# One written order for the whole program of a fused attention and gated MLP kernel, with VectorE and GpSimd placed instruction by instruction and every tile at a written place

## The chip, the cores and the metric

One core of one Trainium2 chip runs the whole program. The metric is the device time of one execution in microseconds (us); the figures for a version are the median, lowest and highest of its runs. The core has five engines that matter here: PE (TensorE; "PEld" are its weight loads, which overlap its matmuls), DVE (VectorE), ACT (ScalarE), POOL (GpSimd), and SP, which issues nearly all transfers between DRAM and on-chip memory. Each engine works its own list of instructions strictly in order; an instruction waits until the data and the places it needs are free, and everything behind it on that engine waits too.

## What is computed

Eight batches with eight heads of dimension 64 hold 512 local and 32 global tokens each. A local token attends to the 32 global tokens and to its local neighbours within 32 positions; a global token attends to all 544. The 4608 results, 512 values each, go through an RMSNorm and a gated MLP with 1536 inner columns:

```python
s_g = scale * q_g @ k_all.T ; out_g = sm(s_g) @ v_all
s_l = concat([scale * q_l @ k_g.T, where(|i-j| <= 32, scale * q_l @ k_l.T, -1e9)])
out_l = sm(s_l) @ concat([v_g, v_l])
xn  = x / sqrt(mean(x * x) + 1e-6) * rms_g
g   = xn @ w_gate ; silu = g * (1 / (1 + exp(-g)))
out = (silu * (xn @ w_val)) @ w_out
```

Inputs and outputs are fp32.

## The kernel before

**Tiles.** The tokens are worked in nine chunks: chunks 0 to 7 are the 512 local tokens of one batch each, chunk 8 is the 256 global tokens. The sigmoid is formed by a tanh. Every large fp32 operand is split into two f16 parts, high and low, so that one product is three f16 matmuls (names `xh`, `xl` for the input, `wf`, `wo` for the weights). Chunks 0 and 1 multiply plainly (`first_chunk`, `moe_f`; matmuls of 128x512 into `p`). Chunks 2 to 7 use a form with seven products in place of eight on quarters of the matrices: `moe_pair` does seven products of 12 matmuls 128x256 for each of six pairs of gate and value columns (into `pq`), `moe_out` the like for the output weight (into `pr`). The combined weights for that are made once, by `fold` and `fold_out`, stored in DRAM (`wd`, `wa`, `wb`) and loaded again for every chunk in tiles `wt` (`fetch`) and `wu` (`fetch_out`).

**Stages.** A head of some 172 us loads and converts the weights, does the attention of chunks 0 and 1 and all of chunk 0's MLP. Then, chunk by chunk, the MLP of one chunk runs on PE, with the attention of a later chunk and the loads of weights between its products. In the head, step names are a letter and a number: L loads a unit (two heads) of q and k, V of v, S scores, M mask and row minimum (DVE), E exponentials (ACT), T transposes (PE), C copies, A values, X division, N and D norm factors, U, H and Y the transposed and split input, I a half product, O the output products. `E5.1` is the exponential of unit 5, half 1. In the chunks, `P24` is the product of work item 24, `R24` what follows it on the other engines, `t` its tail, `w` a load or store, `n` the norm, `O` an output product, and the steps of an attention unit are L, S, M, E, N, F, D, T, V, A, B, X, Y for local tokens (`local_halves`) and GL, GS, GM, GN, GT, GV, GA, GD, GX for global ones (`global_unit`: scores, mask, exponential, transposes, ...).

**Order.** The kernel runs under a manual schedule: what stands earlier in the program stands earlier on its engine. In the head the string `ORDER` lists whole jobs and each is called at once (L1904). For chunks 1 to 8 every step is first recorded (`write`, `doing`), and then replayed by a string for that chunk (`_ORDER_1` to `_ORDER_8`; all calls come from L1929, which is why most rows of the profile name that line). A step is cut into pieces `.0`, `.1` where the engine changes, or at every instruction for the steps R, t and n. So a chunk's steps cannot mix with another chunk's, nor the head's with chunk 1's, and a step of several DVE instructions (a mask, a norm) is one entry.

**Places.** Tiles come from rotating pools, one tag for each kind: `wf` 12 buffers of 128x1024 words, which also hold `wt`, `wu`, `vv` and more, `wo` 7, `h` 6, `st` 6, `v` 4 and so on. The eight PSUM banks are divided by tag too: `pa` 4, `po` 2, `pg` 1, `pv` 1 (`attn_bank` gives one of the four of attention). A new tile waits for the last reader of the one that had its buffer.

## Time and profile before

| | |
|---|---|
| time, median of 3 runs | 920.26 us (919.47 to 922.45) |
| span of the profiled execution | 922.7 us |
| PE busy | 878.8 us, 95% |
| DVE busy | 724.5 us, 79% |
| ACT busy | 556.3 us, 60% |
| POOL busy | 273.2 us, 30% |
| mean DMA rate | 230 GB/s |

The profile holds one execution; the span is its own time, from its first to its last instruction, and no other time of that execution was taken. It lies 2.4 us above the median of the runs. Times in the rows below count from the start of the span. An engine's idle time has a releaser, the instruction or transfer that ended it. PE's granted clock is given as a share of full speed: 1.00 is 2.4 GHz, 0.50 is 1.2 GHz. Where a row of the timeline ends in square brackets, the first number is how long the engine had stood idle before it, and the name behind the arrow is what released it.

### The profile page before, as it was taken

The numbers are of one execution on the slowest core, as the hardware profiler recorded it, in microseconds if no ns is written. First come the engines' busy times: TensorE is split into PE (matmuls) and PEld (weight loads), VectorE is DVE, ScalarE is ACT, GpSimd is POOL, SyncE is SP. The second block draws the span as 40 slices with busy tenths as digits, with TensorE's granted clock in tenths as the row PEclk, the third lists the DMA queues.
The fourth block names the chain that finished last, engine by engine and source line by source line (L and its number), as shares of the span: only waits on it lengthen the run. The fifth ranks groups of instructions, "written<-read, shape, count | busy, mean of one in ns | idle before, by whom it ended". The sixth has DMA issues, their size and how long they took to land.

```text
span 922.7 us, 27756 instructions
## 1 busy us (share of the span) xinstructions
PE 878.8 (95%) x11430; PEld 671.4 (73%) x11430; DVE 724.5 (79%) x1831; ACT 556.3 (60%) x1341; POOL 273.2 (30%) x244
## 2 busy tenths in 40 slices
PE   5699989999999999999999999898999999999998
PEld 4644445544547886588888888787888888888887
DVE  6899998868796887877987888587887897777554
ACT  6899995636452755457565767466575862456132
POOL 0000000032435776306440244122520454133311
PEclk9699989999999999999999999999999999999999
DMA  9983615495377869686677769667876666888665
GB/s 337 405 301 106 192 47 173 130 333 174 90 248 243 274 206 300 194 257 233 206 258 263 245 222 293 198 208 243 265 250 223 206 222 244 247 246 273 215 232 191
DMA packets 101006, 212.03 MB, mean 230 GB/s; under 512 B 8080, under 2 KB 34448, under 8 KB 100880
## 3 DMA queue, kind: packets, MB, share of 16 engines
q1 hardware_dynamic: 100448, 209.94, 69.5%
q8 instruction: 89, 1.46, 0.6%
q10 hardware_dynamic: 432, 0.33, 0.1%
q14 instruction: 37, 0.30, 0.1%
HBM read 183.24 MB, written 27.00 MB: 228 GB/s over the span
## 4 chain that ended last, share of the span: by engine, by line
PE 40%; DVE 5%; DMA 3%; ACT 3%; issue 2%; POOL 1%; DVEq 0%; ACTq 0%; POOLq 0%; SPq 0%
PE pq L1929 20%; PE pr L1929 14%; PE p L1929 3%; DMA wt<-wd 2%; ACT e L1929 1%; PE a L1929 1%; DVE v L1929 1%; DMA wu<-wb 1%; DVE s L1929 1%; DVE u L1929 1%; POOL hs L1929 1%; POOL hu L1929 1%; PE s L1929 1%; ACT s L1929 1%; DVE t L1929 1%
## 5 line engine op out<-in xcount | busy, mean ns | idle before, releaser
L1929 PEld LDWEIGHTS <-wt 128*128 128x128 f16 x3312 | 322.7, 98 | 56.9 <-issue 11.1
L1929 PE MATMUL pq<-xh,wt 128*128 128x256 f16 x1152 | 206.6, 274 | 6.8 <-DMA wt<-wd 2.5
L1929 PE MATMUL pq<-ht,wt 128*128 128x256 f16 x1296 | 158.0, 274 | 2.1 <-POOL ht L1929 1.2
L1929 PE MATMUL pq<-xl,wt 128*128 128x256 f16 x576 | 157.8, 274 | 0.1
L1929 ACT ACTIVATE e<-e,sm 128x128 f32<-128x128 f32 x288 | 104.2, 390 | 27.8 <-DVE sm L1929 27.8
L1929 POOL TENSOR_TENSOR hu<-v,hu 128x256 f16<-128x256 f32 (+1 forms) x60 | 56.5, 958 | 177.6 <-ACT hu L1929 155.1
L1929 PE MATMUL pr<-wu,hs 128*128 128x256 f16 x792 | 92.4, 273 | 0.3 <-DVE hs L1929 0.3
L1929 POOL TENSOR_TENSOR e<-e,sm 128x512 f32<-128x512 f32 x24 | 27.7, 1162 | 205.3 <-DVE sm L1929 205.3
L1929 PEld LDWEIGHTS <-hs 128*128 128x128 f16 x792 | 77.4, 98 | 9.7 <-DVE hs L1929 0.6
L1929 POOL TENSOR_TENSOR hs<-u,hs 128x512 f16<-128x512 f32 x50 | 60.5, 1228 | 65.6 <-ACT hs L1929 37.9
L1929 PE MATMUL pr<-wu,hu 128*128 128x256 f16 x594 | 70.8, 273 | 1.0 <-DMA wu<-wb 0.6
L1929 DVE TENSOR_TENSOR s<-pq,s 128x512 f32<-128x512 f32 x66 | 44.9, 685 | 29.9 <-PE pq L1929 14.1
L1929 ACT ACTIVATE t<-u,half_inv 128x512 f32<-128x512 f32 x72 | 49.6, 717 | 27.0 <-DVE u L1929 23.0
L1929 DVE SCALAR_TENSOR_TENSOR t<-t,u 128x512 f32<-128x512 f32 x72 | 54.0, 758 | 14.4 <-ACT t L1929 14.3
L1929 ACT COPY s<-pq 128x512 f32<-128x512 f32 x72 | 41.3, 580 | 38.3 <-DVE s L1929 18.2
L1929 PEld LDWEIGHTS <-hu 128*128 128x128 f16 x594 | 57.6, 98 | 8.6 <-DMA wu<-wb 0.9
L1929 DVE TENSOR_TENSOR v<-pq,s 128x512 f32<-128x512 f32 x72 | 49.0, 683 | 18.6 <-PE pq L1929 14.8
L1929 PE MATMUL po<-wo,h 128*128 128x512 f16 x288 | 63.4, 379 | 0.0
L1651 PE MATMUL p<-xh,wf 128*128 128x512 f16 x192 | 58.8, 379 | 3.1 <-DVE t L1763 1.2
L1929 PE MATMUL p<-xh,wf 128*128 128x512 f16 x192 | 59.8, 385 | 0.5 <-DVE t L1929 0.5
L1651 PEld LDWEIGHTS <-wf 128*128 128x128 f16 x288 | 27.7, 98 | 37.0 <-issue 3.1
L1929 PEld LDWEIGHTS <-wf 128*128 128x128 f16 x288 | 27.8, 99 | 34.6 <-issue 2.9
(380 smaller groups left out, 1704.7 us busy)
## 6 DMA issues: line engine op xcount, KB each, us to landing
wt<-wd SPq DMA_DIRECT2D x120, 512.0 KB, 5.3
wu<-wb SPq DMA_DIRECT2D x36, 512.0 KB, 5.3
wr<-in_w_in_dram SPq DMA_DIRECT2D x24, 512.0 KB, 8.7
wu<-wa SPq DMA_DIRECT2D x24, 512.0 KB, 4.7
k<-in_qkb_dram SPq DMA_DIRECT2D x24, 448.0 KB, 6.5
gkq<-in_gkq_dram SPq DMA_DIRECT2D x16, 576.0 KB, 7.1
wt<-wd SPq DMA_DIRECT2D x36, 256.0 KB, 4.2
v<-in_vb_dram SPq DMA_DIRECT2D x24, 352.0 KB, 5.6
```

The costliest lines, as they stand in the source:

```text
L1651: nc.tensor.matmul(ps[:, :n], rows[:, a, o : o + P], ch[z][k][:, :n], start=(k == 0 and i == 0), stop=(k == NK - 1 and i == 2),)
L1929: return lambda *a, **k: write(self.engine, lambda: call(*a, **k))
```

## The change

The number of instructions of each kind does not change: 8693 matmuls and transposes, 1543 DVE, 1049 ACT and 240 POOL instructions and 494 transfers from SP are called in both versions. What changes is their order and the places of their tiles.

- The nine tables become one, `ORDER`, over the whole program, with names `chunk:step.n`. The head's steps are recorded and replayed like those of the chunks (chunk number 0), so that any entry may stand anywhere: the head's last work between chunk 1's, a chunk's loads in the chunk before. The old head string stays as `JOBS` and only says in which order steps are recorded.
- Every DVE and every POOL instruction is an entry of its own.
- The pools go. 43 tiles `page` (128x1024 words), 8 tiles `wide` (128x1152) and 8 `banks` are made once, and `tile_of` and `bank_of` take the place of each tile from the written lists `PAGES` and `BANKS`. Any bank may serve any purpose.
- The transposed global weights of `global_unit` are held in two tiles, `pt` and `end`, since one of five parts is longer than a page.
- The scratch for DMA descriptors is set to 2048 bytes (`dynamic_dma_scratch_size`).

The core of the diff; of the tables it shows a piece each:

```diff
-ORDER = """
-z0 L0 S0 M0.0 M0.1 L1 S1 M1.0 E0.0 M1.1 E0.1 T0.1 T0.0 W0 m0 s0 E1.0 C0.0 z1 l0 g0 L2 S2 M2.1 T1.0
+ORDER = """
+0:L0.0 0:S0.0 0:M0.0.0 0:M0.0.1 0:M0.0.2 0:M0.0.3 0:E0.0.0 0:L2.0 0:L3.0 0:M0.1.1 0:M0.1.0 0:M0.1.3
...
-_ORDER_5 = """
-R16.0 N3/2+1.0 w10.0 P18.0 R18.0 t10.3 GV/1+1.0 w13.0 t12.0 t17.1 t18.0 R17.0 D1/2+1.0 V/2+1.0 P19.0
+4:w55.0 4:T1/0+2.0 4:O37.0 4:T3/0+2.0 4:O38.0 4:O39.0 4:n49.1 4:n50.0 4:O40.0 4:R59.0 5:w13.0
...
+PAGES = """
+0c 0a 1a 0a 1a 5a 6a 0a 6a 7a 8a 15a 5a 2a 3a 2a 11a 12a 6c 5a 2c 4a 19a 1c 2c 9a 10a 18a 13a 3a 4a
...
+BANKS = """
+0 1 3 5 0 4 3 2 3 5 3 0 4 1 0 6 2 1 3 4 5 2 1 0 4 4 0 1 5 4 1 5 5 4 2 3 1 0 5 7 2 1 0 5 5 7 6 3 1 7
...
-    pool = ctx.enter_context(tc.tile_pool(name="pool", bufs=2))
+    page = [con.tile([P, 1024], F32, tag=f"page{i}", name=f"page{i}") for i in range(NPAGE)]
+    wide = [con.tile([P, 1152], F32, tag=f"wide{i}", name=f"wide{i}") for i in range(NWIDE)]
+    banks = [psum.tile([P, 512], F32, tag=f"bank{i}", name=f"bank{i}") for i in range(8)]
+    page_at, bank_at, smalls = iter(PAGES.split()), iter(BANKS.split()), [0]
+    def tile_of(shape, dt, name):
...
+        at = next(page_at)
+        if n > 1024:
+            t = wide[int(at[1:])][:, :n]
+        else:
+            of, i = (wide, at[1:-1]) if at[0] == "W" else (page, at[:-1])
+            q = ord(at[-1]) - ord("a")
+            t = of[int(i)][:, q * 256 : q * 256 + n]
...
+    def bank_of(name):
+        return banks[int(next(bank_at))]
...
-            pt = pool.tile([P, 2, 5, P], F32, tag="gpt", bufs=1, name=f"gpt{b}")
+            pt = tile_of([P, 2, 4, P], F32, f"gpt{b}")
+            end = tile_of([P, 2, P], F32, f"gpe{b}")
...
-        t = pool.tile([P, 2, 2, 2, HT], F16, tag="wf", bufs=NF, name=f"wt{c}_{g}{i}")
+        t = tile_of([P, 2, 2, 2, HT], F16, f"wt{c}_{g}{i}")
...
-                st["ps", p] = psum.tile(
-                    [P, 512], F32, tag=bank[p], bufs=2 if bank[p] == "po" else 1, name=f"pq{p}_{g}"
-                )
+                st["ps", p] = bank_of(f"pq{p}_{g}")
...
-        if on and (on != engine or step[0] in "Rtn"):
+        if on and (on != engine or engine in ("vector", "gpsimd") or c and step[0] in "Rtn"):
...
-    for c, plan in plans.items():
-        for name in orders.get(c, plan):
-            for call in plan.pop(name) if c in orders else plan[name]:
-                call()
+    for name in ORDER.split() or list(plan):
+        for call in plan.pop(name):
+            call()
...
-    nc = bacc.Bacc("TRN2", target_bir_lowering=False, num_devices=1)
+    nc = bacc.Bacc("TRN2", target_bir_lowering=False, num_devices=1, dynamic_dma_scratch_size=2048)
```

Three places show how the order moves. The first is ACT in the head, around the exponentials of unit 5 (`E5.1` writes `e_1524`, `E5.0` writes `e_1539`), for which PE's transposes T5.1 and T5.0 wait. Before:

```order
L485 ACTIVATE wr_1475<-wr_1475 128x512
L485 ACTIVATE wr_1477<-wr_1477 128x512
L476 ACTIVATE w17t<-wr_1481 128x512
L476 ACTIVATE w17t<-wr_1483 128x512
L737 COPY pt_1544<-t_1514 128x512
L509 ACTIVATE wq_1555,rowsq<-w16t 128x1024
L509 ACTIVATE wq_1570,rowsq<-w14t 128x1024
L737 COPY pt_1544<-t_1574 128x512
L717 ACTIVATE e_1524,sm_1263<-e_1524,sm_1263 128x128 x4
```

After, `E5.1` is the row on `page_63` and `E5.0` the one on `page_81`; `rowsq` marks the squares of an output weight, 128x1024 each:

```order
L2088 ACTIVATE wide_108<-wide_106 128x512
L2088 ACTIVATE wide_108<-wide_107 128x512
L2088 ACTIVATE page_103<-bank_114,half_inv 128x512
L2088 ACTIVATE page_85<-page_67 128x512
L2088 ACTIVATE page_85<-page_87 128x512
L2088 ACTIVATE page_63,sm_20_181<-page_63,sm_20_181 128x128 x4
L2088 COPY page_72<-bank_116 128x512
...
L2088 ACTIVATE page_76,rowsq<-page_92 128x1024
L2088 ACTIVATE page_80,rowsq<-wide_108 128x1024
L2088 ACTIVATE page_80,rowsq<-page_85 128x1024
L2088 ACTIVATE page_81,sm_20_181<-page_81,sm_20_181 128x128 x4
```

The two squares that stood right ahead of `E5.1` now stand behind it, ahead of `E5.0`, whose own predecessors before were three squares behind `E5.1`.

The second is PE in chunk 1, from the global scores (GS, the rows of 32x272) to their transposes (GT, the rows with `ident`), which need the mask on DVE and the exponential on ACT in between. Before, with 12 matmuls of one gate column between the two:

```order
L1929 MATMUL gs_2275<-gkq_2260 32x272
L1929 MATMUL gs_2277<-gkq_2260 32x272
L1929 LDWEIGHTS wf_1133
L1929 MATMUL p_6_2288<-xh_2169,wf_1133 128x512
...
L1929 MATMUL p_6_2288<-xh_2193,wf_1133 128x512
L1929 MATMUL gt_2295<-ident,ge_2273 112x128 x4
```

After, with three times 12 matmuls, into three banks:

```order
L2088 MATMUL bank_120<-wide_108 32x272
L2088 MATMUL bank_115<-wide_108 32x272
...
L2088 MATMUL bank_114<-page_94,page_65 128x512
...
L2088 MATMUL bank_116<-page_94,page_65 128x512
...
L2088 MATMUL bank_121<-page_94,page_101 128x512
...
L2088 MATMUL bank_120<-ident,wide_108 112x128 x4
```

Two more columns' worth of products moved in between scores and transposes.

The third is SP around the transfer of the weight tile `wt_31` of chunk 5 (entry `w13` of that chunk), which its product P23 reads. Before, behind the global values `gv` of chunk 5's own unit:

```order
L1929 DMA wt_32_3022<-wd_100 128x2x1024
L1929 DMA wt_22_2996<-wd_99 128x2x1024
L1929 DMA wt_23_3006<-wd_99 128x1024
L1929 DMA gv_2987<-in_gv_dram 112x1024
L1929 DMA gv_2988<-in_gv_dram 112x512
L1929 DMA wt_31_3016<-wd_100 128x2x1024
```

After it is the row into `page_88`, ahead of the loads of the global keys and queries (`gkq`) for the unit that is worked in chunk 5:

```order
L2088 DMA page_70<-wd_152 128x2x1024
L2088 DMA page_88<-wd_155 128x2x1024
L2088 DMA wide_109<-in_gkq_dram 128x1152
L2088 DMA wide_110<-in_gkq_dram 128x1152
L2088 DMA page_89<-in_gv_dram 112x1024
```

The transfer moved from the middle of chunk 5 to the end of chunk 4.

## Rows read from the trace of the kernel before

**Rows 1.** The page: busy time of each engine over the span, with its share and its count of instructions, and the granted clock of PE in 40 equal slices, in tenths.

```profile
PE 878.8 (95%) x11430; PEld 671.4 (73%) x11430; DVE 724.5 (79%) x1831; ACT 556.3 (60%) x1341; POOL 273.2 (30%) x244
PEclk9699989999999999999999999999999999999999
```

**Rows 2.** Busy time by stretch: from and to in us, length, then busy us (and instructions begun) of PE, PE's weight loads, DVE, ACT and POOL, the granted clock, the DMA engines' busy share and GB/s. The first four stretches are the head, the next chunk 1, the last chunk 7.

```profile
0.00:44.00 44.00, 27.16 (x601) 23.44 (x602) 32.42 (x148) 33.90 (x100) 0.20 (x4) 0.77 0.98 370
44.00:112.00 68.00, 64.87 (x493) 31.48 (x493) 67.31 (x137) 65.70 (x104) 0.00 (x0) 1.00 0.61 205
112.00:132.00 20.00, 15.50 (x235) 9.16 (x234) 17.85 (x64) 18.29 (x43) 0.00 (x0) 0.83 0.25 90
132.00:172.00 40.00, 40.00 (x491) 22.95 (x492) 33.76 (x80) 24.29 (x63) 0.00 (x0) 1.00 0.34 113
172.00:286.00 114.00, 110.67 (x1184) 55.09 (x1165) 90.80 (x241) 56.59 (x168) 40.83 (x32) 0.99 0.68 210
783.00:874.00 91.00, 90.95 (x1012) 79.86 (x1010) 65.35 (x130) 41.39 (x72) 29.58 (x28) 1.00 0.77 243
```

**Rows 3.** PE's longest waits, summed by line and releaser: us in total, times, longest.

```profile
PE x00t L1110 <- DVE dg L1104: 6.3, 1, 6.3
PE s L688 <- DMA k<-in_qk_dram: 6.1, 1, 6.1
```

**Rows 4.** PE's timeline in the head, start and length in us: the transposes T5.1 and T5.0.

```profile
120.17 1.48 PE L732 MATMUL t<-ident,e 128*128 128x128 f32 x4 [3.05 <-ACT e L717]
128.38 0.92 PE L732 MATMUL t<-ident,e 128*128 128x128 f32 x4 [1.12 <-DVE sm L702]
```

**Rows 5.** PE's timeline in chunk 1: the transposes GT.

```profile
208.92 0.76 PE L1929 MATMUL gt<-ident,ge 128*112 128x128 f32 x5 [2.34 <-ACT ge L1929]
209.94 0.82 PE L1929 MATMUL gt<-ident,ge 128*112 128x128 f32 x5 [0.26 <-ACT ge L1929]
```

**Rows 6.** PE's timeline, the waits of over 0.3 us for a weight transfer in chunks 2 to 8: P41 of chunk 4, P23 and P33 of chunk 5, O18 of chunk 8.

```profile
550.88 1.49 PE L1929 MATMUL pq<-ht,wt 128*128 128x256 f16 x12 [0.65 <-DMA wt<-wd]
627.14 0.39 PE L1929 MATMUL pq<-xh,wt 128*128 128x256 f16 x1 [2.21 <-DMA wt<-wd]
643.75 0.28 PE L1929 MATMUL pq<-xh,wt 128*128 128x256 f16 x1 [0.31 <-DMA wt<-wd]
910.49 0.72 PE L1929 MATMUL pr<-wu,hu 128*128 128x256 f16 x5 [0.64 <-DMA wu<-wb]
```

**Rows 7.** PE's timeline, the waits of over 0.3 us for another engine's work in chunks 1 to 5 (GT's apart): in order, a product of chunk 1, P30 of chunk 2, P3 and P29 and O36 of chunk 3, P19 of chunk 4, P4 of chunk 5.

```profile
183.41 0.38 PE L1929 MATMUL p<-xh,wf 128*128 128x512 f16 x1 [0.47 <-DVE t L1929]
333.14 0.27 PE L1929 MATMUL pq<-xh,wt 128*128 128x256 f16 x1 [0.65 <-DVE u L1929]
391.45 0.81 PE L1929 MATMUL pq<-ht,wt 128*128 128x256 f16 x6 [1.24 <-POOL ht L1929]
434.31 0.27 PE L1929 MATMUL pq<-xh,wt 128*128 128x256 f16 x1 [1.45 <-ACT u L1929]
483.85 0.93 PE L1929 MATMUL pr<-wu,hu 128*128 128x256 f16 x7 [0.38 <-DVE oo L1929]
518.48 0.27 PE L1929 MATMUL pq<-xh,wt 128*128 128x256 f16 x1 [1.25 <-DVE s L1929]
595.39 0.27 PE L1929 MATMUL pq<-xh,wt 128*128 128x256 f16 x1 [0.32 <-DVE s L1929]
```

**Rows 8.** PE's timeline in chunk 5: the values of a local unit, behind a wait that the trace gives no releaser.

```profile
587.86 0.42 PE L1929 MATMUL a<-et,v 32*64 32x64 f32 x21 [2.18 <-issue]
```

**Rows 9.** The five stretches behind the head's first 44 us in which PE's granted clock was 0.50, columns as in rows 2.

```profile
121.80:125.20 3.40, 3.40 (x128) 2.89 (x112) 2.19 (x14) 3.40 (x11) 0.00 (x0) 0.50 0.03 5
128.60:132.00 3.40, 3.40 (x11) 1.50 (x10) 3.33 (x7) 2.80 (x6) 0.00 (x0) 0.50 0.18 71
210.50:213.90 3.40, 3.40 (x34) 1.43 (x39) 0.86 (x3) 1.54 (x4) 0.00 (x0) 0.50 0.57 160
589.40:592.80 3.40, 3.40 (x18) 2.36 (x17) 0.30 (x1) 1.32 (x4) 0.00 (x0) 0.50 0.99 266
626.90:630.30 3.40, 3.16 (x15) 2.24 (x16) 0.31 (x1) 3.35 (x14) 0.51 (x1) 0.50 0.99 295
```

**Rows 10.** ACT's timeline ahead of T5.1: the last square of an output weight, then the first exponential of E5.1.

```profile
118.10 1.06 ACT L509 ACTIVATE wq<-w14t 128x1024 bf16<-128x1024 f32 x1
119.61 0.42 ACT L717 ACTIVATE e<-e,sm 128x128 f32<-128x128 f32 x1
```

**Rows 11.** The chain of work that ended last, a piece of it: start, length, what; 13 products of 12 matmuls in a row on PE.

```profile
518.48 17.38 PE pq L1929 x156
```

**Rows 12.** The page's list of transfers (KB each, median us from issue to landing), for the weight tiles.

```profile
wt<-wd SPq DMA_DIRECT2D x120, 512.0 KB, 5.3
```

**Rows 13.** DVE's and POOL's timeline in chunk 2: a DVE instruction with two on-chip operands beside POOL, the two of POOL that it met, a DVE instruction that reads PSUM beside POOL, and the first form again where POOL did nothing.

```profile
336.96 1.27 POOL L1929 TENSOR_TENSOR s<-s,s 128x512 f32<-128x512 f32 x1
337.24 1.54 DVE L1929 SCALAR_TENSOR_TENSOR t<-t,u 128x512 f32<-128x512 f32 x1
338.19 2.58 POOL L1929 TENSOR_TENSOR od<-os,od 128x1024 f16<-128x1024 f32 x1
339.33 0.65 DVE L1929 TENSOR_TENSOR u<-pq,s 128x512 f32<-128x512 f32 x1
298.35 0.68 DVE L1929 SCALAR_TENSOR_TENSOR t<-t,u 128x512 f32<-128x512 f32 x1
```

More of the change, by code (lines that the diff above doesn't have):

```diff
@@ L794, in load @@
             if w == 0:
-                late["mask"] = con.tile([P, 6 * P], F32, tag="mask", name="maskb")
+                late["mask"] = tile_of([P, 6 * P], F32, "maskb")
                 nc.sync.dma_start(late["mask"], maskb)
@@ L885, in scores @@
             st["et"] = [
-                pool.tile([P, 1088], F32, tag="k", name=f"et{u}{x}") for x in range(2)
+                tile_of([P, 1088], F32, f"et{u}{x}") for x in range(2)
             ]
@@ L1374, in products @@
             hi, lo = ch["op"][p]
-            first = p in bank
+            first = p in own
             for j in range(2):
```

839 lines of the change are left out of this document (487 added, 352 removed), and 8 rows, old and new, of the table BANKS.

## Prediction

> **What bounds the kernel now.** I read the page first. PE is busy 95% of the span and no other engine over 80% [rows 1]; since the change keeps every matmul, the most that it can give back is what PE stands idle, 922.7 − 878.8 = 43.9 us, and what PE loses where its clock is low. Busy time by stretch then says where the idle time lies [rows 2]: 16.8 us in the first 44 us, 3.1 us to 112 (68 less 64.87), 4.5 us from 112 to 132, none from 132 to 172, 3.3 us in chunk 1, and at the end almost none: chunk 7 runs at 90.95 of 91 us. So chunks 6 and 7 have nothing to give, the head and chunks 1 to 5 something. [...]
>
> PE's waits and its timeline give the single stalls. Two large ones stand at the start: 6.1 us for the first keys and 6.3 us for a norm factor of chunk 0 [rows 3]. Then 3.05 us ahead of T5.1 and 1.12 us ahead of T5.0 [rows 4], 2.34 and 0.26 us ahead of the global transposes of chunk 1 [rows 5], four waits for weights [rows 6], seven for another engine [rows 7], and one of 2.18 us without a releaser [rows 8]. The granted clock is the third source: behind the start it fell to 1.2 GHz in five stretches [rows 9], each with PE busy for all or nearly all of its 3.4 us, so each did 1.7 us' worth of work at 2.4 GHz and cost about 1.7 us. Each follows one of the stalls above: in order T5.1, T5.0, GT, the wait of 2.18 us, and P23's 2.21 us. I count such a stretch as gone when its stall goes.
>
> **The change, part by part.** Only order and places change; I priced every instruction in both orders at the mean of its shape in this trace and compared what stands ahead of each waiting instruction on its engine. All terms are against the profiled execution's span, 922.7 us, which lies 2.4 us above the median of 920.26; I carry the sum to both.
>
> *A, unit 5 in the head.* Before T5.1, ACT ran two squares of 1.06 us each and only then E5.1 [rows 10]; they now stand behind it. All told ACT's work ahead of E5.1 falls from 105.8 to 95.9 us, but ahead of E5.0 only from 110.5 to 108.3. T5.0 comes behind T5.1 on PE with the same PE work ahead of it (97.9 us in both), so what T5.1 gains beyond E5.0's own 2.2 us is waited for again at T5.0. Late next is E5.0. Bounds: 0, since DVE is 90% and ACT 91% busy there [rows 2], and −7.6, both stalls and both clock stretches (4.17 + 3.4). I take −2.2, E5.0's own advance, and leave the stretches, since half of the idle time stays.
>
> *B, global transposes of chunk 1.* GT waited for ACT's exponential behind 12 matmuls of 128x512. Matmuls of 128x256 run at 17.38 / 156 = 0.111 us each where nothing waits [rows 11]; twice that for 512 columns makes 12 of them 2.7 us. The time from scores to transposes was then 2.7 + 2.6 = 5.3 us. Now 36 matmuls, 8.0 us, stand between. The stall should go with its clock stretch: −4.3 (2.6 + 1.7). Bounds 0 (the mask, now split into entries, falls behind other DVE work) and −4.3. The cover is those three products; without them the 2.6 us return.
>
> *C, weight transfers.* The four waits sum to 0.65 + 2.21 + 0.31 + 0.64 = 3.81 us [rows 6]. A tile of 512 KB lands 5.3 us after its issue [rows 12]. I counted PE's work between a transfer's entry and its first product: 63 of 222 transfers had under 5.3 us before, 2 of 221 have now, and the median went from 8.0 to 42.5 us. For the four that waited it went 0.1 to 13.1, 2.7 to 43.3, 0.1 to 37.7 and 6.0 to 74.7. A free place must exist that early, and SP's queue is in order, so a transfer that waits for its page holds those behind it; with 8 to 40 us in hand that is survivable. −5.5, the waits and P23's clock stretch; bounds 0 and −5.5.
>
> *D, engines that were late.* The seven waits sum to 0.47 + 0.65 + 1.24 + 1.45 + 0.38 + 1.25 + 0.32 = 5.76 us [rows 7]. The time table is meant for these: a DVE instruction with two on-chip operands took 1.54 us beside two of POOL and 0.68 us alone, while one that reads PSUM took 0.65 us beside POOL [rows 13]. Only the DVE and POOL waits can come from that; the 1.45 us stood behind ACT's own queue. I take half, −2.9; bounds 0 and −5.8.
>
> *E, the wait without releaser* (2.18 us and its clock stretch [rows 8, 9]): nothing in the order tells its cause, so 0; bounds 0 and −3.9.
>
> *F, the start:* the norm factor's chain (row sums, scale, spread) is the same length, and its DVE work ahead 0.7 us shorter (26.9 to 26.2): 0, bounds −2 and +1. Its loads end as before, so the 6.1 us for the keys stay.
>
> *G, banks.* With eight free banks in place of 4 + 2 + 1 + 1, a bank is not always given back earlier. I counted PE work between the last product into a bank and the first into the next tile there: of 525 such turns 44 left under 1.4 us before, 65 do now. Six of the waits above (all of [rows 7] but POOL's) were such turns: 4.52 us, so 0.103 us for each of the 44. 21 more cost +2.2; bounds 0 and the rival below.
>
> Sum: −2.2 − 4.3 − 5.5 − 2.9 + 2.2 = −12.7, that is 910.0 for an execution like the profiled one, **907.6 us** for the median.
>
> [...] By [rows 13] a DVE instruction beside POOL was longer by 0.86 us, less than POOL's 1.27. [...]
>
> **Rivals.**
> 1. *The table only moves the wait.* If DVE is held anyway for as long as POOL works, standing the two in turn frees no time on DVE: the products' results come out of the banks as late as before, and D is 0. For it: in [rows 13] POOL's 1.27 us had 0.99 left when DVE began, and DVE's 0.68 grew by 0.86, nearly a full wait. Against: an order can put PSUM readers, which lose nothing, beside POOL. 907.6 + 2.9 = **910.5**. [...]
> 2. *More goes.* The wait of 2.18 us (E, 3.9) and the rest of A's stalls with one clock stretch (4.17 − 2.2 + 1.7 = 3.7) go too, and the banks cost nothing (2.2): 907.6 − 9.8 = **897.8**. For it: nothing else bounds PE behind 172 us. Against: DVE's and ACT's load in the head.
> 3. *The idle time returns elsewhere, or the order on paper does not hold on the chip:* the head's middle is bound by DVE (17.85 of 20 us [rows 2]), transfers wait for pages rather than for their turn, and gaps as large as the old ones open at other products. **920 ± 2.**
> 4. *Slower: bank turns.* Place: the products of `moe_pair` and `moe_out`, one every 1.34 us (12 x 0.111), each of which needs a bank that DVE or ACT must have read out. The order was made from durations written in a table; where DVE runs an instruction late, the 65 tight turns all wait, and since DVE is now fixed instruction by instruction, nothing else of its own can fill in. Price: mean of the six, 4.52 / 6 = 0.75 us. It decides from 20 more waiting turns on (14.9 / 0.75, the gains of A to D); if half of the 65 wait, 24.4 us against 4.5 paid now, +19.9 − 14.9 = +5: **925**. For it: more tight turns than before, and a table rests on durations, where one form took 0.68 or 1.54 us [rows 13]. Against: 38 of 44 did not wait.
>
> **How the numbers follow.** A difference of 0.3% (2.8 us) is about what a measurement can tell. Forecast 0.39, rival 1 0.15, rival 2 0.10, rival 3 0.15, rival 4 0.21. The first three are faster by over 0.3%: 0.64; rival 3 is the same: 0.15; rival 4 slower: 0.21. The range goes from 897, just below rival 2 (the bounds of A to E together, 27.1, would give 893), to 926, just above rival 4 with half of the tight turns waiting; its worse outcomes and all bounds at once are left out, under 2 in 10. Faster cases alone span 897 to 917.
>
> **What would show it.** Right: PE busy about as before (879 us) and idle near 31 us; no wait of over 1 us at GT in chunk 1; no wait for `wt` or `wu`, and only two or three low-clock stretches behind the head. A is right if T5.1 follows without a wait and T5.0 with at most 1 to 2 us. D is right if waits of PE for DVE and POOL in chunks 2 to 5 sum to 3 us or less, rival 1 if they stand near 6. Rival 4 shows as many waits of 0.3 to 1.5 us ahead of `pq` and `pr`, released by DVE or ACT reading a bank; rival 3 as idle time in the head's middle of as much as before. I would be wrong outright if low-clock stretches became more without stalls, or if PE's busy time itself grew.

## The result, and the profile after

The change made the kernel slower, not faster. Nine runs of it gave a median of **926.04 us** (922.5 to 930.11), nine of the kernel before on the same chip 919.99 us (917.27 to 922.45). The ratio is 1.0072, with a 95% interval of 1.0053 to 1.0091. 907.6 us was forecast, and 926.04 lies just above the range, 897 to 926.

The profiled execution of the change has a span of 924.4 us and took 926.16 us, about its median. That of before has a span of 922.7 us; runs of before add 2.1 us around the span, so it took some 4.8 us more than the median of 919.99. The two profiles therefore differ by 1.7 us where the medians differ by 6, and the ledger below accounts for the 1.7.

The page of after, to be read beside [rows 1]:

```profile
PE 877.3 (95%) x11430; PEld 670.8 (73%) x11430; DVE 706.2 (76%) x1831; ACT 552.5 (60%) x1341; POOL 268.3 (29%) x244
PEclk8699999999999999999999999999998999999999
```

PE's work is the same, and DVE does its own in 18.3 us less. PE's idle time is 924.4 − 877.3 = 47.1 us where it was 43.9 and I wanted some 31. Where it lies, in the waits of PE summed by line and releaser (us in total, times, longest):

```profile
PE bank L2088 <- issue: 20.0, 10, 4.5
PE bank L2088 <- DVE page L2088: 9.6, 8, 5.7
PE bank L2088 <- DMA page<-in_qk_dram: 6.4, 2, 5.8
PE bank L2088 <- ACT page L2088: 2.4, 5, 0.9
PE bank L2088 <- DVE kk L2088: 1.6, 1, 1.6
PE bank L2088 <- DMA page<-wb: 0.2, 1, 0.2
```

The first line is the case. In 20 us PE stood before an instruction for which the trace has no releaser: no semaphore of an engine and no data transfer. Before, the like was one wait of 2.18 us [rows 8], one of 1.21 us in the head and one of 0.26 us in chunk 1. PE's timeline shows the sites, two in the head and eight from chunk 2 on (two of these, of 0.4 and 0.5 us, are left out), and with them the matmuls that stand ahead of the longer wait of the head, and the wait for the norm factor:

```profile
14.85 0.47 PE L2088 MATMUL bank<-page,page 64*32 64x128 f32 x8 [1.74 <-issue]
27.45 1.79 PE L2088 MATMUL bank<-page,page 128*32 128x64 f32 x106
33.29 0.86 PE L2088 MATMUL bank<-page,page 128*32 128x64 f32 x22 [4.05 <-issue]
42.50 7.71 PE L2088 MATMUL bank<-page,page 128*128 128x128 f32 x102 [5.66 <-DVE page L2088]
...
293.98 0.61 PE L2088 MATMUL bank<-wide 64*32 64x272 f32 x2 [0.82 <-issue]
355.12 2.24 PE L2088 MATMUL bank<-page,page 64*32 64x128 f32 x41 [1.46 <-issue]
444.44 0.43 PE L2088 MATMUL bank<-wide,page 32*64 32x64 f32 x22 [3.02 <-issue]
584.70 0.65 PE L2088 MATMUL bank<-wide,page 32*64 32x64 f32 x25 [2.32 <-issue]
614.70 1.54 PE L2088 MATMUL bank<-page,page 64*32 64x128 f32 x25 [1.14 <-issue]
695.25 4.85 PE L2088 MATMUL bank<-page,page 128*128 128x256 f16 x22 [4.55 <-issue]
```

All that waited for `issue`, but the last, are small fp32 matmuls of the attention, and the last stands directly behind a run of such matmuls. The norm factor (the row at 42.50) is the wait of 6.3 us in [rows 3]; the wait shrank to 5.66 us, but its matmul starts at 42.50 where it started at 37.98 before.

The stretches, with the columns of [rows 2]; the last three are those at half clock:

```profile
0.00:48.00 48.00, 27.82 (x627) 23.77 (x635) 31.68 (x144) 33.53 (x99) 0.20 (x4) 0.75 0.98 381
112.00:132.00 20.00, 18.12 (x265) 9.65 (x264) 19.60 (x60) 19.94 (x44) 0.00 (x0) 1.00 0.58 189
132.00:176.00 44.00, 43.59 (x521) 24.58 (x520) 38.54 (x103) 24.76 (x69) 1.53 (x1) 1.00 0.33 104
444.80:448.20 3.40, 3.40 (x22) 2.42 (x18) 1.09 (x3) 3.06 (x5) 1.77 (x3) 0.50 0.62 184
584.80:588.20 3.40, 3.40 (x39) 2.50 (x39) 1.36 (x3) 1.17 (x3) 0.00 (x0) 0.50 0.22 51
694.00:700.80 6.80, 4.85 (x22) 3.04 (x21) 0.66 (x1) 0.67 (x2) 0.00 (x0) 0.50 1.01 301
```

The reader should see three things. The head's middle went from 15.50 to 18.12 us busy and no longer loses clock: the two stretches at half clock there [rows 9] are gone. The other three of [rows 9] are gone too. But three new ones stand right behind the waits at 444, 584 and 695 us, one of double length.

What half clock costs is in the trace of before: f16 matmuls of one shape followed each other, in the median, every 109 ns (128x256) and 216 ns (128x512) at a granted clock of 1.00, and every 213 and 427 ns at 0.50. So 256 more columns take 107 and 214 ns, which is 2.4 and 1.2 columns a nanosecond. Taken as one column a clock, an estimate, these are the 2.4 and 1.2 GHz told ahead of the result; the trace itself gives the clock as a share. A stretch of 3.40 us, all busy, costs 1.7 us by that.

The ledger of PE's idle time, from the two traces (the head ends at 46 us here, the chunks begin at 176 us):

| us | before | after |
|---|---|---|
| head to 46 | 16.8 | 20.2 |
| 46 to 176 | 7.6 | 5.4 |
| chunks, no releaser | 2.5 | 14.5 |
| chunks, all other | 13.4 | 3.4 |
| behind the last matmul | 3.5 | 3.5 |

The ledger counts every gap; the views leave out gaps of 0.15 us and less, so 14.2 us stand there for the 14.5.

The change took 10.0 us out of the chunks' waits for engines and transfers, as it was made to. It put 12.0 us of another kind in.

**What that kind is.** The page has a queue that moves instructions, with the same row in both versions (packets, MB, share of 16 engines):

```profile
q8 instruction: 89, 1.46, 0.6%
```

Its 89 packets are of 16,384 bytes each. PE has 2 x 11,430 = 22,860 records, weight loads and matmuls; 22,860 / 89 = 257. So I take a packet for a block of about 256 of PE's instructions, 64 bytes each, an estimate from these counts. The waits without a releaser end at one distance from the landing of such a block (us, from the packet records of the traces):

| trace | block begins | takes | lands | wait ends | later by |
|---|---|---|---|---|---|
| before | 585.54 | 0.98 | 586.52 | 587.86 | 1.34 |
| after | 442.11 | 0.96 | 443.07 | 444.44 | 1.37 |
| after | 582.15 | 1.31 | 583.45 | 584.70 | 1.25 |
| after | 692.57 | 1.23 | 693.80 | 695.25 | 1.45 |

I read this as PE out of its own instructions, and the count bears it out. Number PE's instructions from the start, with the 74 to 87 records of its sequencer (semaphores, drains) counted in, and the blocks from 0. Then every wait of PE without a releaser in the sixteen traces of this case, 101 in all, stands ahead of instruction 449 + 256k, and ends 1.2 to 1.6 us after block k has landed. So I conclude that block k begins with that instruction, and that PE waits there until it is in.

How far ahead a block is asked for is not in the trace. None of the two traces' blocks began to move earlier than 297 instructions ahead of its own first one; with some time for the request I estimate from that 297 that it is asked for some 310 instructions ahead. All times from request to landing below are estimates that rest on this point. The block lands a median of 4.4 us after it in the chunks (a tenth of them over 6.4 us; before 4.3 and 6.2).

A product of `moe_pair` is 24 instructions in 1.34 us, so 310 instructions last 17 us, and nothing shows. But A or B of a local unit is 160 instructions, S 256, and 22 matmuls with their loads pass in 0.43 us (the row at 444.44). The five longest stalls of the chunks lie in a run of S (355.12, 614.70), or in or right behind A and B set next to each other (444.44, 584.70, 695.25); the other three, 0.4 to 0.8 us, stand where B follows A, or the global scores follow B, with some products between. In the head the stall of 1.74 us lies in S of unit 1, with S of units 2 and 3 in a row before it, and that of 4.05 us in A of unit 2, which now stands directly behind A of unit 1 (106 + 22 matmuls in the rows at 27.45 and 33.29).

The longest of the waits, the one whose block began at 692.57 us, fell where the data queue was full (the DMA queues of after in 690.5 to 695 us; q1 moves the data):

```profile
q1 hardware_dynamic: 438, 1.18, 102.5%
q8 instruction: 1, 0.02, 1.7%
```

### The profile page after: what moved, and what is told of

It is laid out like the page before. It is cut to its first block, busy times and chain, and to the rows that moved or that the text cites. A ratio compares the mean times of both kernels' runs of the same rounds, so it can differ in the third digit from the quotient of the medians.

```text
span 924.4 us, 27869 instructions
## 1 busy us (share of the span) xinstructions
PE 877.3 (95%) x11430; PEld 670.8 (73%) x11430; DVE 706.2 (76%) x1831; ACT 552.5 (60%) x1341; POOL 268.3 (29%) x244
## 5 line engine op out<-in xcount | busy, mean ns | idle before, releaser
L2088 PE MATMUL bank<-page,page 128*128 128x256 f16 (+5 forms) x8000 | 745.4, 285 | 29.7 <-issue 13.4
L2088 PEld LDWEIGHTS <-page 128*128 128x128 f16 (+1 forms) x5478 | 528.0, 98 | 182.9 <-issue 17.0
L2088 POOL TENSOR_TENSOR page<-page,page 128x512 f16<-128x512 f32 (+5 forms) x179 | 201.6, 1146 | 402.6 <-ACT page L2088 344.3
L2088 ACT CAST page<-page 128x512 f16<-128x512 f32 (+1 forms) x157 | 122.0, 798 | 92.9 <-DVE page L2088 88.9
L2088 DVE TENSOR_TENSOR page<-bank,page 128x512 f32<-128x512 f32 x158 | 106.4, 684 | 69.5 <-PE bank L2088 44.0
L2088 ACT COPY page<-bank 128x512 f32<-128x512 f32 (+3 forms) x165 | 85.9, 541 | 113.0 <-PE bank L2088 90.7
L2088 ACT ACTIVATE page<-page,sm 128x128 f32<-128x128 f32 x352 | 129.0, 390 | 31.0 <-DVE sm L2088 29.2
L2088 DVE TENSOR_TENSOR page<-page,page 128x256 f32<-128x256 f32 (+5 forms) x170 | 100.3, 604 | 11.4 <-ACT page L2088 7.3
L2088 PE MATMUL bank<-wide,page 32*64 32x96 f32 (+7 forms) x2310 | 83.0, 265 | 6.1 <-issue 5.8
L2088 ACT ACTIVATE page<-page 128x512 f32<-128x512 f32 (+2 forms) x92 | 76.5, 894 | 13.0 <-DVE page L2088 10.5
L2088 DVE CUSTOM_DVE_ANT_0 page<-bank,page 128x128 f32<-128x128 f32 x256 | 62.1, 286 | 24.1 <-PE bank L2088 20.4
L2088 PEld LDWEIGHTS bank<-wide,page 32*64 32x64 f32 (+2 forms) x2016 | 32.4, 128 | 13.4 <-issue 9.8
```

The costliest lines, as they stand in the source:

```text
L2088: return lambda *a, **k: write(self.engine, lambda: call(*a, **k))
```

## Experiments

My theory: PE runs out of instructions where small matmuls stand close together (place), and the longer the more data is under way when the block is fetched (latency). Rival a: the waits come from something tied to one step of the program. Rival b: the descriptor scratch, which the change sets too. Rival c: the weight transfers do it alone, by their number. Ratios are against the kernel before on the same chip. The times that the theory expected were met in experiments 2 and 3 and missed by 0.2 us in the last one. In all the others the measured time lies outside them; where the waits without releaser went down as expected, other waits came in their place.

**1. Shift the blocks.** Small matmuls that nothing reads, ahead of the total of the head: 48 in the change, 64 in the kernel before. They move all later instructions against the block boundaries and change no order.

```diff
+pad = f32(ones).bitcast(BF16)[:, :P]
+for _ in range(48):
+    nc.tensor.matmul(gp[0][:, 0:1], pad, pad[:, 0:1], start=True, stop=True)
```

> The changed kernel with 48 tiny matmuls (128x1, bf16, with their weight loads 96 PE instructions) put in front of one small matmul of the head, where PE idles 1.6 us; their result is overwritten. At 0.025 us a pair in the trace they cost 1.2 us at most. Theory CODE: PE's own instructions are brought by DMA in blocks of 16 KB, 256 instructions of 64 bytes, 89 blocks in either trace on queue 8; where a run of small attention matmuls uses a block up faster than the next one lands, PE waits, and the trace calls it issue. All 8 waits called issue of over 0.4 us in chunks 1 to 8 (14.2 us) end 1.3 to 1.4 us after a block has landed, and stand 379 to 405 instructions behind a multiple of 256 counted from that block. Then 96 instructions more move the grid of blocks against the program: by the trace's own times of request and landing the waits go from 14 to about 6 us and to other places (the largest near 293 us, 2.7, and near 545 us, 1.5), and two to four of the four stretches at 1.2 GHz behind them go (1.7 us each). Time 926 - 8 - 3.4 to 6.8 + 1 = 912 to 916 us. Theory PLACE: the waits belong to the steps at which they stand (a bank, a place or a transfer whose release the trace does not show): the same instructions wait as long as before, 926 to 928 us.

> The kernel before with 64 such tiny matmuls (128 PE instructions, 1.6 us) at the same matmul of the head. CODE: the kernel before happens to stand well on the grid of blocks; half a block further the waits in chunks 1 to 8 go from 2.2 to about 24 us by the trace's own times (the largest 4.7 near 292 us, 3.5 near 584, 3.1 near 480, 2.9 near 187, 2.8 near 685), with some five stretches at 1.2 GHz of 1.7 us. Time 920 + 20 to 30 = 940 to 948 us. PLACE: 920 to 922 us, one wait of 2.2 us at the same values step of chunk 5.

The change with 48: 923.11 us, 1.0041 (1.0025 to 1.0057), between the 912 to 916 of the theory and the 926 to 928 of rival a. Of the waits that ended at 444, 584 and 614 us none is left and of that at 695 us 0.6 us, but others of 0.6 to 2.1 us end at 294, 454, 566, 660 and 754 us. They sum to 9.0 us where I had forecast 6, and one more of 2.7 us, ending at 548 us and put down to ACT, stands ahead of instruction 449 + 256k too. All other gaps in the chunks rose from 3.4 to 7.2 us, and four stretches at half clock stand behind the head. Before with 64: 930.22 us, **1.0114 (1.0082 to 1.0146)**, less than the 940 to 948 forecast. Its waits of PE, and the longest in the timeline:

```profile
PE a L1932 <- issue: 6.0, 2, 4.1
PE pq L1932 <- issue: 4.3, 5, 1.8
PE pr L1932 <- issue: 3.0, 3, 1.9
```

```profile
196.36 0.42 PE L1932 MATMUL a<-et,v 32*64 32x32 f32 x3 [4.08 <-issue]
```

13.4 us of waits without releaser in the chunks against 2.5, in a kernel with the old order, and the one of [rows 8] gone. 64 tiny matmuls, 1.6 us of work, cost some 10.6 us. That removes rival a, and since the transfers of data are the same, rival c as well.

**2. The scratch for descriptors** alone, in the kernel before:

```diff
-nc = bacc.Bacc("TRN2", target_bir_lowering=False, num_devices=1)
+nc = bacc.Bacc("TRN2", target_bir_lowering=False, num_devices=1, dynamic_dma_scratch_size=2048)
```

> The kernel before with the descriptor scratch of 2048 bytes that the change brings, and nothing else of it. Theory SCRATCH: the small scratch slows the issue of transfers (landing times of weights rose from 5.3 to 6.3 us), and with it the arrival of instructions: 923 to 926 us. CODE and PLACE: the transfers from SP do not use it, 918 to 922 us.

921.39 us, 1.0005 (0.9976 to 1.0033): no effect shows, and rival b falls; whether SP's transfers use the scratch at all is not shown. Its profile (span 919.4 us) is a second execution of the old order: 3.4 us of such waits in the chunks, and two stretches at half clock behind the head where the first had five. Its waits were as long (up to 2.2 us without releaser and 2.6 us for a weight, against 2.18 and 2.21), but the granted clock is 1.00 in each stretch of 100 us from 300 us on, where the first has 0.98 from 500 to 600 and from 600 to 700 us. So a stall of 2 to 3 us does not lower the clock in every execution.

**3. Less data under way.** Chunks 2 to 7 load one half of each `wt` tile; the products read that half twice, so the other half of the weights is left out.

```diff
-nc.sync.dma_start(t[:, :n], wd[g][:, o : o + d * (n - 1) + 1 : d])
+nc.sync.dma_start(t[:, :n, 0], wd[g][:, o : o + d * (n - 1) + 1 : d, 0])
...
-w[:, j, i, k * P : (k + 1) * P],
+w[:, 0, i, k * P : (k + 1) * P],
```

> The changed kernel with the weight transfers of chunks 2 to 7 half as long: of each tile the second half of the columns is left out, and the products use the first half twice, so PE's work keeps its count and shapes. CODE: blocks of instructions land late because data transfers fill the same DMA engines (their busy share was 0.9 to 1.0 between request and landing of the late ones); with a quarter less to move in the chunks they land earlier, the waits called issue fall from 14 to under 5 us and the stretches at 1.2 GHz from four to at most one. Time 911 to 917 us. PLACE: no wait hangs on the data transfers' load, 925 to 927 us.

914.28 us, 0.9942 (0.9922 to 0.9961). The median from request to landing fell from 4.4 to 3.4 us, the waits in the chunks (from 176 us on) from 14.2 to 8.0 us where under 5 were expected, and one stretch at half clock is left:

```profile
PE bank L2091 <- issue: 8.0, 5, 2.8
```

So data under way is nearly half of it: five waits stay at the same places. Place and latency both count; data alone, rival c, does not hold here either.

**4. Hold transfers back.** Each SP transfer from chunk 1 on waits until the third-last, or the second-last, load has landed (a transfer of one element out of that tile goes ahead of it in SP's queue); a third version does so in the head too.

```diff
+x = landing[-3]
+now.sync.dma_start(marks[x.dtype][:, n : n + 1], one)
 call(to, src)
```

> The changed kernel, in which from chunk 1 on each transfer from SP is preceded by a transfer of one element out of the tile that the third load before it filled, so SP waits until that load has landed and at most three loads are under way. In the two traces a block of PE's instructions took 2.6 to 3.0 us from request to landing with one or two transfers under way and 4.9 to 5.3 with five or more. CODE: the blocks land earlier, the waits called issue in chunks 1 to 8 fall from 14 to about 5 us, the stretches at 1.2 GHz from four to one or two: 926 - 9 - 4 = 911 to 915 us, as long as no weights come late. Against it: loads that are held come late, and PE waits for DMA instead (0.5 to 2 us each): up to 926.

> The same with at most two loads under way. CODE: request to landing of an instruction block falls to about 3 us in the chunks, the waits called issue to under 3 us, at most one stretch at 1.2 GHz behind the head: 926 - 11 - 5 = 910 us where no data comes late; with two loads of 512 KB under way the rate may fall under the 229 GB/s that the kernel moves on the mean, then weights come late and the time lies between 912 and 930 us.

> The first of these with the head included: at most three loads under way from the start. CODE: in the head too blocks of instructions come late behind the weight loads (waits called issue of 1.74 and 4.05 us before 34 us, where the kernel before has 1.2): both together fall under 2 us, and the first transposed input of chunk 0 (which started at 42.5 us, at 38.0 in the kernel before) starts near 39 us; 3 to 5 us better than with the chunks alone: 907 to 911 us. If the head is bound by the loads themselves, holding them costs as much as it brings: as with the chunks alone, 911 to 915 us.

940.63 us (1.0228), 1037.38 us (1.1285) and 965.53 us (1.0503). The theory expected 907 to 915 us. With three under way the waits without releaser fell to 7.8 us from 176 us on, where 5 were expected, but PE waited for late engines in their place:

```profile
PE bank L2104 <- DVE page L2104: 8.2, 8, 4.9
PE bank L2104 <- issue: 7.8, 3, 4.1
PE bank L2104 <- ACT page L2104: 6.4, 5, 2.5
PE bank L2104 <- DVE wide L2104: 2.9, 1, 2.9
```

Ahead of the longest of these, 4.9 us, DVE itself had waited 6.9 us for a transfer. With two, weights (`wd`) were waited for in 36.2 us. In these three runs a bound on all transfers cost far more than it gave.

**5. Undo A and B of the prediction.** E5.1 goes back behind the last two squares, and four half products move behind GT in chunk 1.

> The changed kernel with two places of the order put back: E5.1 behind two squares of output weights on ACT (2.1 us), and two half products (24 matmuls) instead of six between the global scores and transposes of chunk 1, the other four behind the transposes. By the prediction's steps A and B: T5.1 stands behind E5.0 now, which is not moved, so the first place costs 0 to 1 us; at the second a wait of about 2 to 2.6 us with a stretch at 1.2 GHz (1.7 us) comes back: +3.5 to +5 us, 929 to 931 us. Other theory: these waits are covered by other work now, and PE stands just as long elsewhere: 925 to 927 us.

928.11 us, 1.0109 (1.0066 to 1.0151). Against before on each chip that is 9.3 us over where the change was 6.1 over, so some 3 us more, where 3.5 to 5 were expected; the two intervals overlap, and the time alone doesn't settle it. GT waits again:

```profile
206.92 1.30 PE L1768 MATMUL bank<-ident,wide 128*112 128x128 f32 x10 [1.32 <-ACT wide L1768]
```

Half of the wait in [rows 5], 2.6 us, came back with the four products. For E5.1 nothing shows: between 46 and 176 us PE is idle 5.8 us against 5.4. A stretch at half clock is back at 124 us, but the change with 48 matmuls has one there too, so it can't be put down to E5.1.

**6. Move the small matmuls apart.** Entries of the order are moved and nothing else: twelve steps S, A or B with what hangs on them (`after_space`); the first 183 entries of the head in the old order (`after_head`); both.

One of the twelve, A of unit 0 in chunk 2's part of the table, as pieces of the order:

```diff
-3:P2.0 3:P1.0 2:R59.0
+3:P2.0 2:R59.0 2:A/0+2.0 3:P1.0
...
-3:R1.1 2:A/0+2.0
+3:R1.1
```

> The changed kernel with nothing added or left out: in the order, twelve runs of small attention matmuls (nine steps A or B of the values, 160 PE instructions each, and four scores steps S, 256 each, less one) are moved by one to five products so that no two stand close behind each other; with them moves only what depends on them, 31 of 3692 entries. All eight stretches in which PE ran out of instructions hold A, B or S: in each some 310 instructions went by in under 6 us, where a block takes 4.5 to 6 us from request to landing and 1.4 us more. CODE: with the trace's own durations put in the new order and a block at 5.5 us the eight waits shrink from 14 to 2 us in all (at most 4), three or four of the four stretches at 1.2 GHz go (1.7 us each): 926 - 10 to 13 - 5 to 7 = 906 to 911 us. Other theory, DATA: the values wait for transposed exponentials that the trace does not name; standing earlier they wait longer, 926 to 930 us.

> The changed kernel with the first 183 entries of its order (to the transposed inputs of chunk 0) put back into the order of the kernel before, as far as the written places allow. Before, the scores of units 0 to 3 stood spread between other steps; in the change those of three units stand in a row (384 PE instructions), and PE ran out of code at 13.1 and 29.0 us (1.74 and 4.05 us). CODE: both waits together fall under 2 us, the first transposed input starts near 38 to 39 us instead of 42.5, and the time falls by 3 to 5 us, 921 to 923. Other theory: the head's middle is bound by DVE and ACT (97 and 99% busy between 44 and 112 us before), the head start does not reach chunk 1: 925 to 927 us.

> Both edits. CODE: their gains add, 902 to 908 us, under the 919.5 us of the kernel before. If the head's start is lost in its middle: as with the first alone, 906 to 911 us.

933.56 us (1.0163), 939.1 us (1.0212) and 948.79 us (1.0323). 902 to 911 us were expected for the first and the last and 921 to 923 for the second. In the first the cause is nearly gone from the chunks, and the time is up all the same. Its waits from 176 us on:

```profile
PE bank L2086 <- DVE page L2086: 12.8, 15, 3.1
PE bank L2086 <- ACT page L2086: 4.7, 6, 2.1
PE bank L2086 <- DVE sm L2086: 1.9, 1, 1.9
PE bank L2086 <- issue: 1.4, 1, 1.4
```

14.2 us of waits without releaser became 1.4, and 2.9 us for DVE and ACT became 19.4. The written order of DVE is fixed instruction by instruction, so I read this as steps of PE that are moved and hold up what DVE has behind them; experiment 7 takes one of them back. The head in the old order has lost its two waits, but its loads of keys come late (13.0 us for `in_qk` in its waits of PE, 6.4 in the change), and in the chunks 17.5 us of waits without releaser stand where 14.2 did. The rest of its time is not split here.

**7. A few moves.** Six steps only, each by one to three products; then without the one that was late for DVE (A of unit 2 in chunk 3).

Three of the five, as they stand in the tables: S of unit 0 (chunk 2) one product later, A and B of unit 0 (chunk 4) one later, A of unit 0 (chunk 5) three earlier and so away from its B.

```diff
-2:P45.0 2:S/0+2.0 3:w10.0
+2:P45.0 3:w10.0
...
+2:t38.1 2:P50.0 2:S/0+2.0 2:N0/0+2.0
...
-4:O41.0 4:A/0+2.0 4:n49.2 4:R62.0 4:R53.0 4:B/0+2.0 4:n52.0 5:Y/0+1.0
+4:O41.0 4:n49.2 4:R62.0 4:R53.0 4:n52.0
...
+5:w3.0 5:P2.0 4:A/0+2.0 4:B/0+2.0 5:Y/0+1.0
...
-5:n48.1 6:P7.0
+5:n48.1 5:T2/0+2.0 5:T0/0+2.0 5:A/0+2.0 6:P7.0
```

> The changed kernel with six of the small-matmul steps moved, each by one to three products, and of what depends on them only what must go along (at most four other entries, no step of VectorE or GpSimd but two transposes, a mask and three copies): A of unit 2 in chunks 2 and 3 (one and two products earlier), S of chunk 2 and of chunk 5 and A with B of chunk 4 (one product later), A of unit 0 in chunk 5 (three earlier). CODE: the waits called issue in chunks 1 to 8 go from 14 to about 5 us (those at 353, 582, 613 and 691 us gone or under 0.8, that at 441 us from 3.0 to about 2), three of the four stretches at 1.2 GHz go, and new waits for DVE or ACT come to at most 2 us, since twelve moves brought 15 us of them but mostly where transposes and masks were moved in DVE's list: 926 - 9 - 5 + 2 = 912 to 916 us. Against it: any move of a small step makes a later step late by as much, 923 to 928 us.

> The six moves without that of A in chunk 3, which in the last run waited 2.89 us for DVE itself, made a product 11 us later wait 3.15 us, and brought two stretches at 1.2 GHz. Five small steps move, by one to three products. CODE: the wait of 3.0 us at 441 us with its stretch comes back, the two of 2.89 and 3.15 us with theirs go: 920.5 - 6.0 - 3.4 + 3.0 + 1.7 = 915 to 917 us; of the four stretches of the change one is left. Against it: the run of six gained for another reason than the code waits, 919 to 922 us.

Six moves: 920.51 us, 1.0002 (0.9983 to 1.002). Five: **919.09 us, 0.9979 (0.9967 to 0.9992)**. It lies 1.6 us under before on its chip where the change lay 6.1 over, a difference of 7.6 us. The waits without releaser in the chunks are 5.6 us (14.5 before the moves), of which 3.1 stand at the site that was left alone; all other gaps there rose from 3.4 to 7.3 us, and the time at half clock behind the head fell from 13.6 to 6.8 us: −8.9 + 3.9 − 3.4 = −8.4 us where the spans differ by −7.9. From six moves to five the two waits of 2.89 and 3.15 us for DVE went and the one of 3.1 us came back, as expected, but with a stretch at half clock of double length; 919.09 is outside the 915 to 917 expected, and lies in the 919 to 922 of the other theory, whose own reason, that the moves gained by something else, the waits do not bear out.

**8. The five moves, and a hold in the head alone.** The head's loads of raw weights (steps W) and of V keep four under way at most.

```diff
+if self.engine == "sync" and at_work[0] == 0 and at_work[1][0] in "WV":
+    return lambda *a, **k: write("sync", lambda: held(call, *a))
...
+now.sync.dma_start(mark[:, n : n + 1], landing[-4][0:1, 0:1].bitcast(I32))
 call(to, src)
```

> The same with the loads of weights and values in the head held so that at most four of them (512 KB each) are under way: ahead of each stands a transfer of one element out of the tile of the fourth before it. CODE: in the head blocks took 7 to 13 us from request to landing behind 1.0 busy DMA engines; with some 2 MB under way about 6; the waits called issue at 13.0 and 28.5 us (1.8 and 4.0) fall under 2 us together, the first transposed input starts 2 to 4 us before 41.7 us, and the time is 2 to 4 us under that of the five moves alone. Other theory: the head needs its weights as early as they come; held, they make PE and DVE wait, and the time is the same or longer.

**914.91 us** (914.05 to 915.81), 0.9944 (0.9927 to 0.9961): 0.6% under the kernel before and so under both kernels, and 4.2 us under the five moves alone. PE's timeline at three sites:

```profile
29.36 0.54 PE L2098 MATMUL bank<-page,page 128*32 128x64 f32 x22 [0.87 <-issue]
...
39.07 7.09 PE L2098 MATMUL bank<-page,page 128*128 128x128 f32 x99 [5.63 <-DVE page L2098]
439.50 0.65 PE L2098 MATMUL bank<-wide,page 32*64 32x64 f32 x23 [3.26 <-issue]
```

The wait of 4.05 us in the head (3.98 with the five moves alone) became 0.87, the norm factor's matmul starts at 39.07 where it stood at 42.50 (41.92), and the head's time at half clock is 17.0 us (23.9 in the change, 20.4 before and with the five moves). The third and fourth block landed an estimated 5.4 and 6.0 us after their request, 8.8 and 9.8 in the change. The site at 439 us is the one that nothing here removed without a price.

**The count that goes with it.** For every block that is fetched in the chunks I took the time that PE needed for the 310 instructions behind the request, its idle time left out. How many of them took less than 6 us, and less than 5, stands beside the waits. The counts hang on the estimated point of the request: taken five instructions earlier or later, single ones change by up to four.

| kernel | under 6 us | under 5 us | waits without releaser, chunks, us |
|---|---|---|---|
| before | 7 | 1 | 2.5 |
| after | 9 | 4 | 14.5 |
| before, 64 matmuls | 15 | 7 | 13.4 |
| after, 48 matmuls | 9 | 3 | 9.0 |
| five moves | 8 | 2 | 5.6 |
| twelve moves | 1 | 0 | 1.6 |

## Why the prediction was wrong

**What bounds the kernel** was read rightly: PE, its idle time and its clock. What went wrong is that I counted the causes of idle time that the trace named, and one that it did not name grew nearly sixfold.

**A, unit 5:** right in place, and larger. T5.1 and T5.0 (the rows at 123.80 and 126.48) wait for nothing where they did [rows 4]; in their place stand 1.63 us for `kk` and 0.41 us for ACT:

```profile
123.55 0.38 PE L2088 MATMUL bank<-kk,ones 128*128 128x1 f32 x2 [1.63 <-DVE kk L2088]
123.80 0.64 PE L2088 MATMUL bank<-ident,page 128*128 128x128 f32 x4
126.48 0.66 PE L2088 MATMUL bank<-ident,page 128*128 128x128 f32 x4
```

Between 46 and 176 us the idle time fell by 2.2 us, the term's own figure, but both stretches at half clock went as well, which I had left standing: 2.2 + 3.4 = 5.6 us. Two things are not shown: that the gain is E5.0's advance, since experiment 5 undid E5.1 alone; and that both stretches belong to the order, since the second execution of the old order has one of the two.

**B, GT:** right; wait and stretch are gone [rows 5, 9], and undoing it brought 1.32 us of the wait back:

```profile
209.70 1.26 PE L2088 MATMUL bank<-ident,wide 128*112 128x128 f32 x10
```

**C, weight transfers:** right. No wait of over 0.3 us for a weight is left where there were four, 3.81 us [rows 6].

**D, late engines:** right. 5.76 us [rows 7] became 2.6 us in five waits of 0.4 to 0.8 us, a gain of 3.2 where I took 2.9:

```profile
531.27 0.92 PE L2088 MATMUL bank<-page,page 128*128 128x256 f16 x7 [0.51 <-DVE page L2088]
592.23 1.03 PE L2088 MATMUL bank<-page,page 128*128 128x256 f16 x8 [0.38 <-ACT page L2088]
700.88 0.92 PE L2088 MATMUL bank<-wide 64*32 64x272 f32 x24 [0.79 <-DVE page L2088]
715.45 0.81 PE L2088 MATMUL bank<-page,page 128*128 128x256 f16 x6 [0.41 <-DVE page L2088]
745.76 0.93 PE L2088 MATMUL bank<-page,page 128*128 128x256 f16 x7 [0.50 <-ACT page L2088]
```

Rival 1 said that the table would only move the wait on DVE; DVE is busy 18.3 us less, and the time in which DVE and POOL are busy together went from 201.2 to 182.6 us. In the trace of before the 12 DVE instructions of the form in [rows 13] that met over 0.2 us of POOL's work took a median of 1.04 us, the 57 that met none 0.68; for those that read PSUM (`u<-pq,s`, 128x512) it was 0.69 us both for 22 beside POOL and for 11 without. What makes this difference no run shows.

**G, banks:** wrong in sign. All five of the waits above ended when a DVE or ACT instruction had read a bank (`page<-bank` in the trace), so they are turns of a bank as I meant them: 2.59 us in five where the six before had 4.52 us. Tight turns rose from 44 to 65 and the waits at them fell, so a price per tight turn does not hold; the +2.2 has no place in the sum, and the gain stands under D. Rival 4, which rests on the price, did not come.

**E, the wait without a releaser, is the step that failed.** I wrote that nothing in the order tells its cause, took 0 and let the bounds run from 0 to −3.9: I allowed that it goes, not that it spreads. By the count above it was PE out of instructions: the wait of [rows 8] stands ahead of instruction 449 + 256 x 56, like the rest. Its kind went from 2.5 to 14.5 us and brought three stretches at half clock, one of them double, for the one that it had. At half the clock (213 ns a matmul in place of 109) those were busy 11.65 us with what would be 5.8, so they cost some 5.8 us where the old one cost 1.7: with the waits 12.0 + 4.1 = +16.1. The order did tell it, once its cause is known: A and B next to each other, S in a row, 160 and 256 instructions a step.

**F, the start, failed for the same cause.** I priced the norm factor's chain of work and took 0 with +1 as the worse end; A of units 1 and 2 now stand in a row on PE while the weights load at a DMA share of 0.98, the block lands an estimated 9 us after its request, and PE waits 4.05 us. S of units 2, 3 and 1 gave the 1.74 us before it. The factor's matmul starts 4.5 us later than before; the idle time of the head is 3.4 us more.

**The sum.** A to D gave 5.6 + 10.0 (all other waits in the chunks) + 3.4 (B's and C's stretch) = 19.0 us, more than the 14.9 forecast. E and F took 16.1 + 3.4 = 19.5 us. That is +0.5 by terms where the spans differ by +1.7; the rest I did not split. That the medians differ by 6 and these two executions by 1.7 I put down to the execution of before, a long one of its kind. Against the second execution of the old order (experiment 2, 919.4 us, nearer the median) the change is 5.0 us longer: 1.1 us more idle time, since 11.1 us more without a releaser and 3.1 in the head stand against 11.7 us less of the chunks' other waits and 1.4 less between 46 and 176 us; and 3.9 us more of PE busy, with 37.5 us of the span at half clock against 27.3. Taking part of the cause away gave its part back: the five moves 7.6 us, the hold in the head 4.2 us more. So the cause of the stalls is shown by experiment, in the chunks and in the head; how the 6 us of the medians divide between the two is open.

I had named as outright wrong "if low-clock stretches became more without stalls". They became fewer, each behind a stall. None of the four rivals was this case. Rival 3 came nearest in words, since idle time returned elsewhere, but by a cause it did not hold.

## What to carry to other kernels

A wait that the trace gives no releaser had a cause here, and a change of order took it from 2.5 to 14.5 us: find its cause before a term of 0 is written, and bound it upward as well. Where an engine runs many short instructions, count them: here the change had nine runs of some 310 of PE's instructions (an estimate) in under 6 us and 14.5 us of waits, the twelve moves one such run and 1.6 us. An order that looks better by every data wait can put two short runs side by side. With DVE written out by single instructions, twelve moves of PE's steps to mend this cost more than they gave; five, chosen by what DVE had behind them, paid.

## What the runs showed that I had not expected

- By the counts above PE's instructions come in blocks of 16,384 bytes (89 packets of q8), each begins at instruction 449 + 256k, and PE goes on 1.2 to 1.6 us after a late block has landed. The estimated time from request to landing was up to 2.4 us for the quickest tenth in the chunks, over 6.4 us for the slowest, and some 8 to 12 us for the second to fourth block in the head of the change, with the DMA engines 98% busy.
- 64 matmuls of one column that nothing reads, put into the head, made the kernel 1.1% slower, by where the block boundaries then fell: the waits there went from 2.5 to 13.4 us.
- The old order had five stretches at half clock behind the head in one profiled execution and two in another (there with the descriptor scratch of 2048 bytes), with about the same stalls.
- A bound of two loads under way made the kernel 13% slower; the same kind of bound on a few loads at the start made it faster.
